# An SSM and feed-forward mix on one core: the sine tables' span angles moved into the table instructions, turns of x over two PSUM banks, and another order for emptying the last turn

## The chip, the cores and the metric

The kernel runs on one core of one Trainium2 chip. The metric is the device time of one execution in microseconds (us). One profiled execution of each kernel leaves a trace. The span in a trace is about 1.8 us shorter than the device time of the same run (214.0 against 215.83 us), since it goes from the first to the last instruction.

Engines: PE is TensorE (matmuls), DVE is VectorE, ACT is ScalarE.

## The reference

```python
def reference(x, ...):                       # x: 2048 x 640
    g = sigmoid((x * gate_w).sum(-1))
    # A: a diagonal state space model with complex poles
    Lam_bar = exp(dt * Lam)                  # dt = exp(log_dt), 640 poles
    h[t] = Lam_bar * h[t-1] + B_bar @ x[t]   # 2048 steps
    a = 2 * Re(h @ C.T) + x * Dskip
    # B: a feed-forward block, 640 -> 1728 -> 640
    b = gelu(x @ w1 + b1) @ w2 + b2
    return g * a + (1 - g) * b
```

The kernel does the scan in a rotating frame. For that it needs tables of sine and cosine of `angle * t` for t from 0 to 511, and the sine and cosine of five single angles ("spans": 1, 512, 256, 128, 64 steps; 25 columns, since the 640 poles lie in five blocks of 128) to double the tables and to carry the state between chunks.

## The kernel before

Only the opening, about the first 15 of 214 us, is touched. It must turn (transpose) the first 512 rows of x by matmuls with an identity matrix (the later rows are turned by loads that transpose). There are four row blocks of 128 rows and five column blocks each. A turn writes PSUM, and VectorE or ScalarE empties it into `xT[0]`. In between, TensorE runs strips of the first feed-forward product, into six PSUM banks. With eight banks in all, two are left for turns: `pA` and one spare.

```python
def turn_first(a, other):              # column blocks 0 and 1 of row block a
    t = bank()                         # the spare bank
    turn(t, 0, a, 0);            turned(nc.vector, t, 0, a, 0, 1)
    turn(other, a * P, a, 1);    turned(nc.scalar, other, a * P, a, 1, 2)

def turn_rest(a, t, *parts):           # column blocks 2, 3, 4 of row block a
    for k in range(KA, KD):            # KA = 2, KD = 5
        turn(t, (k - KA) * P, a, k)
    for engine, k0, k1 in parts:
        turned(engine, t, (k0 - KA) * P, a, k0, k1)

def part(kd, a):                       # a strip: six matmuls of 128 columns
    strip(kd, a * P, (a + 1) * P, kd == 0)

part(0, 0)
turn_first(1, pA)
part(1, 0)
part(0, 1)
turn_first(2, pA)
part(1, 1)
turn_first(3, pA)
part(0, 2)
turn_rest(0, bank(), (nc.scalar, KA, KD))
part(1, 2)
# ... cut: angles per step, dt and thp_c, from small columns
part(0, 3)
turn_rest(1, bank(), (nc.vector, KA, KD))
part(1, 3)
turn_rest(2, pA, (nc.scalar, KA, KD))
part(2, 0)
turn_rest(3, bank(), (nc.vector, KA, KA + 1), (nc.scalar, KA + 1, KD))
# the first 64 steps of the tables: u = t * angle, reduced to half a turn
nc.vector.tensor_tensor(out=u, in0=tf[...], in1=over(thp_c[:], HC), op=ALU.mult)
# ... cut: kk = round(u), red = u - kk
part(2, 1)
part(2, 2)
part(2, 3)
nc.scalar.activation(out=FS[:, :, 0:HC], in_=red, func=ACT.Sin, scale=TWO_PI_M)
# ... cut: cosine; then the same five steps for the 25 span angles (two, kq, redq, absq, sq, cq)
for kf in range(FA):
    for kd in (4, 3):
        ff1_mm(banks[kf], 0, kf, kd, 0, CH, False, 3)   # 512 columns each
for kf in range(FA):
    ff1_act(banks[kf], 0, kf)                           # Gelu: the table is loaded anew
```

`turn_rest(3, ...)` is the one turn that two engines empty. The first engine named goes first.

## Time and profile before

| | before |
|---|---|
| time, median of 3 runs (range) | 215.72 us (215.24 to 215.78) |
| span of the trace | 214.0 us |
| first turn / last matmul starts | 3.29 / 211.06 us |
| Sin table load / first Gelu start | 10.03 / 13.88 us |

The page's first part, of before: busy time, share of the span, number of instructions.

```profile
PE 210.5 (98%) x1407; PEld 126.5 (59%) x1407; DVE 189.4 (88%) x389; ACT 103.3 (48%) x188; POOL 1.0 (0%) x13
```

TensorE is the bound, but "busy" cannot show how well it is fed, since matmuls are pipelined and their ends overlap with the next ones' starts. The starts can. Below is the timeline of TensorE in the opening of before: start in us, busy us, line, operation, shape, count.

```profile
4.57 0.42 PE L233 MATMUL bank<-ident,xn 128*128 128x128 bf16 x2
4.79 1.18 PE L267 MATMUL bank<-xT,w1a 128*128 128x128 bf16 x12
5.80 0.28 PE L233 MATMUL bank<-ident,xn 128*128 128x128 bf16 x2
5.91 0.50 PE L267 MATMUL bank<-xT,w1a 128*128 128x128 bf16 x6
6.40 0.27 PE L233 MATMUL bank<-ident,xn 128*128 128x128 bf16 x2
6.51 0.50 PE L267 MATMUL bank<-xT,w1a 128*128 128x128 bf16 x6
7.00 0.33 PE L233 MATMUL bank<-ident,xn 128*128 128x128 bf16 x3
...
9.11 2.46 PE L267 MATMUL bank<-xT,w1a 128*128 128x128 bf16 x24
11.41 0.17 PE L404 MATMUL bank<-ident,prmB 128*128 128x18 bf16 x1
```

Line 233 is a turn, line 267 a strip. Single matmuls of 128 columns start 55.6 ns apart here once the clock is full, those of 512 columns 215.8 ns apart. So six of them from 5.91 us should let the next start at 6.24. It starts at 6.40: TensorE stood for 0.155 us. No view of waits lists this, because the pipelined ends hide it. In the same way the row of 24 (eighteen of 128 columns, six of 512, though the row is labelled by its first) takes 18 x 0.0556 + 6 x 0.2158 = 2.30 us, and 11.41 - 9.11 is just that: no wait. The two turns at 4.57 are 0.107 us apart, twice as much: the clock is still at half speed, until 5.52 us in this run.

ScalarE in before, the same columns, with the idle time ahead of an instruction and what ended it in brackets:

```profile
8.78 0.49 ACT L242 ACTIVATE xT<-bank 128x384 bf16<-128x384 f32 x1 [0.18 <-PE bank L233]
9.63 0.38 ACT L242 ACTIVATE xT<-bank 128x256 bf16<-128x256 f32 x1 [0.37 <-DVE xT L240]
10.03 1.28 ACT L392 ACT_TABLE_LOAD   x1
11.33 0.47 ACT L392 ACTIVATE hs<-gel 128x320 f32<-128x320 f32 x1
...
12.59 1.28 ACT L272 ACT_TABLE_LOAD   x1
13.88 0.69 ACT L272 ACTIVATE gel<-bank,colB 128x512 bf16<-128x512 f32 x1
```

The second line is the last turn: ScalarE waits until VectorE has taken its piece out of the same bank. VectorE in before:

```profile
9.31 0.29 DVE L240 CAST xT<-bank 128x128 bf16<-128x128 f32 x1 [0.42 <-PE bank L233]
9.52 0.48 DVE L386 TENSOR_TENSOR gel<-tf,thp_c 128x320 f32<-128x320 f32 x1
...
11.33 0.18 DVE L395 TENSOR_TENSOR two<-thp_c,spans 128x25 f32<-128x25 f32 x1
11.54 0.18 DVE L397 CAST kq<-two 128x25 int32<-128x25 f32 x1
11.76 0.18 DVE L398 TENSOR_TENSOR redq<-two,kq 128x25 f32<-128x25 f32 x1
11.97 0.18 DVE L399 SCALAR_TENSOR_TENSOR absq<-redq 128x25 f32<-128x25 f32 x1
```

The last four are the span angles, which the change takes away.

### The profile page before, as it was taken

What the parts mean: (1) busy time and instruction counts of PE and PEld (TensorE: products, weight loads), DVE (VectorE), ACT (ScalarE), POOL (GpSimd) and SP (SyncE); (2) the same over time, 40 slices, a digit from 0 to 9 for tenths busy, and PEclk for the clock granted to TensorE, in tenths of its full rate; (3) what the DMA queues carried; (4) which work ended last, traced back from release to release, by engine and by line L of the source; (5) the groups of instructions that cost most, each with busy time, mean ns of one, the idle gap of its engine ahead of it and who ended that gap; (6) DMA issues with size and microseconds to landing.
All of it is one profiled execution on the core that took longest, in us unless ns stands there. A gap on an engine that the chain in (4) does not pass through costs nothing.

```text
span 214.0 us, 3599 instructions
## 1 busy us (share of the span) xinstructions
PE 210.5 (98%) x1407; PEld 126.5 (59%) x1407; DVE 189.4 (88%) x389; ACT 103.3 (48%) x188; POOL 1.0 (0%) x13
## 2 busy tenths in 40 slices
PE   8999999999999999999999999999999999999994
PEld 5945444454475644775457777444457687676773
DVE  2599999999998999999999999999999999993153
ACT  3599956675759579203573210455683422305100
POOL 1000000000000000000000000000000000000000
PEclk9999999999999999999999999999999999999999
DMA  6879999999000000052000006100000000110011
GB/s 192 222 178 190 201 156 246 347 207 230 1 0 0 3 0 0 14 152 96 0 0 3 0 0 180 68 0 2 3 0 14 0 3 31 61 34 0 0 66 61
DMA packets 31571, 15.84 MB, mean 74 GB/s; under 512 B 22978, under 2 KB 31554, under 8 KB 31554
## 3 DMA queue, kind: packets, MB, share of 16 engines
q1 hardware_dynamic: 30850, 14.99, 29.7%
q10 hardware_dynamic: 704, 0.62, 0.9%
q8 instruction: 11, 0.18, 0.4%
q14 instruction: 6, 0.05, 0.1%
HBM read 7.48 MB, written 2.62 MB: 47 GB/s over the span
## 4 chain that ended last, share of the span: by engine, by line
PE 98%; DVE 0%; issue 0%
PE bank L267 27%; PE bank L614 27%; PE bank L673 20%; PE bank L555 20%; PE bank L230 1%; PE bank L630 1%; PE bank L293 1%; PE bank L233 1%; DVE ot L678 0%; PE bank L362 0%; PE bank L283 0%; PE bank L404 0%; PE bank L373 0%
## 5 line engine op out<-in xcount | busy, mean ns | idle before, releaser
L614 PE MATMUL bank<-w_sb,gel 128*128 128x384 bf16 (+1 forms) x416 | 57.9, 300 | 0.0
L614 PEld LDWEIGHTS <-gel 128*128 128x128 bf16 x416 | 40.2, 98 | 17.1 <-issue 0.8
L558 ACT ACTIVATE bu<-bank 128x512 bf16<-128x512 f32 x40 | 23.7, 606 | 37.6 <-PE bank L555 37.6
L272 ACT ACTIVATE gel<-bank,colB 128x512 bf16<-128x512 f32 x52 | 33.6, 695 | 10.5 <-PE bank L267 10.2
L673 PEld LDWEIGHTS <-hs 128*128 128x128 bf16 x330 | 31.7, 98 | 11.7
L509 DVE TENSOR_TENSOR_SCAN g<-r_c,carry,v 128x512 bf16<-128x512 f32 x30 | 37.2, 1270 | 0.0
L622 ACT ACTIVATE gb<-bank,gcol 128x384 f32<-128x384 f32 (+1 forms) x32 | 15.1, 526 | 32.8 <-PE bank L614 16.6
L267 PE MATMUL bank<-xT,w1a 128*128 128x512 bf16 (+1 forms) x174 | 28.5, 319 | 0.0
L673 PE MATMUL bank<-CT_im,hs 128*128 128x320 bf16 (+2 forms) x165 | 27.1, 295 | 0.0
L673 PE MATMUL bank<-CT_re,hs 128*128 128x320 bf16 (+2 forms) x165 | 27.1, 295 | 0.0
L678 DVE SCALAR_TENSOR_TENSOR ot<-bank,gcol,gb 128x320 bf16<-128x320 f32 (+2 forms) x33 | 17.4, 533 | 9.8 <-PE bank L673 9.5
L555 PE MATMUL bank<-xT,BT_re 128*128 128x512 bf16 x100 | 24.9, 379 | 0.0
L555 PE MATMUL bank<-xT,BT_im 128*128 128x512 bf16 x100 | 24.9, 379 | 0.0
L267 PEld LDWEIGHTS <-w1a 128*128 128x128 bf16 x174 | 14.9, 101 | 11.6
L267 PE MATMUL bank<-xT,w1b 128*128 128x512 bf16 x80 | 17.9, 379 | 0.0
L555 PEld LDWEIGHTS <-BT_im 128*128 128x128 bf16 x100 | 9.8, 98 | 11.8
L588 DVE TENSOR_TENSOR bank<-xn,Dbc 128x320 f32<-128x320 bf16 (+2 forms) x33 | 14.5, 482 | 2.1 <-ACT gb L622 2.1
L555 PEld LDWEIGHTS <-BT_re 128*128 128x128 bf16 x100 | 9.6, 98 | 11.0
L490 DVE TENSOR_TENSOR v<-wa,wb 128x512 bf16<-128x512 bf16 x40 | 15.2, 421 | 0.6
L603 ACT ACTIVATE bank<-b2bc 128x384 f32<-128x384 bf16 (+1 forms) x24 | 11.7, 526 | 7.6 <-DVE ot L678 7.6
L490 DVE TENSOR_TENSOR wa<-TCOS,g 128x1024 bf16<-128x1024 bf16 x20 | 13.7, 686 | 0.1
L267 PE MATMUL bank<-xT,w1c 128*128 128x512 bf16 x60 | 13.7, 379 | 0.0
(103 smaller groups left out, 167.8 us busy)
## 6 DMA issues: line engine op xcount, KB each, us to landing
out_dram<-ot SPq DMA_DIRECT2D x15, 160.0 KB, 1.8
w_sb<-in_B_w_dram SPq DMA_DIRECT2D x1, 2080.0 KB
xn<-in_A_x_dram SPq DMA_DIRECT2D x3, 640.0 KB
w1b<-in_B_w_dram SPq DMA_DIRECT2D x5, 128.0 KB, 3.8
w1c<-in_B_w_dram SPq DMA_DIRECT2D x5, 112.0 KB, 4.3
w1a<-in_B_w_dram ACTq DMA_DIRECT2D x2, 192.0 KB, 3.0
w1a<-in_B_w_dram SPq DMA_DIRECT2D x1, 384.0 KB, 3.5
xn<-in_A_x_dram SPq DMA_DIRECT2D x4, 64.0 KB, 3.7
```

Of the source, the lines that this page charges most:

```text
L267: nc.tensor.matmul(p[:, t0:t1], lhsT=w, rhs=xT[c][:, kd, t0:t1], start=(kd == 0) if first is None else first, stop=(kd == last), skip_grou ...
L272: nc.scalar.activation(out=gel[c][:, kf, :], in_=p[:, :], func=ACT.Gelu_apprx_tanh, bias=b1_c[:, kf:kf + 1])
L490: nc.vector.tensor_tensor(out=o, in0=a, in1=b, op=op)
L509: nc.vector.tensor_tensor_scan(s["g"][:, ri, :], r_c[:, ks:ks + 1].to_broadcast([P, CH]), s["v"][:, ri, :], init, ALU.mult, ALU.add)
L555: nc.tensor.matmul(p[:], lhsT=BT[ks >= KSA][:, kd, (ks % KSA if ks < KSA else ks - KSA) * P:][:, 0:P], rhs=xT[c][:, kd, :], start=(kd == 0 ...
L558: nc.scalar.activation(out=bu[:, ri, :], in_=p[:], func=ACT.Identity)
L588: dve_now(ck.pe, 0.45, lambda: nc.vector.tensor_tensor(out=p[:, 0:d1 - d0], in0=xn[c][:, a, d0:d1], in1=Dbc[:, d0:d1], op=ALU.mult))
L603: nc.scalar.activation(out=v, in_=src, func=ACT.Identity)
L614: nc.tensor.matmul(p[:, col:col + d1 - d0], lhsT=gel[c][:, kf, a * P:(a + 1) * P], rhs=w2_sb[:, kf, d0:d1], start=False, stop=False, skip_ ...
L622: nc.scalar.activation(out=gbs[ti][:, d0:d1], in_=p[:, col:col + d1 - d0], func=ACT.Identity, scale=gcol[:, 1, ti:ti + 1])
L673: nc.tensor.matmul(p[:, 0:d1 - d0], lhsT=hs[c][:, j, lo:lo + P], rhs=CT[:, j % KS, d0:d1], start=False, stop=(j == 2 * KS - 1), skip_group ...
L678: nc.vector.scalar_tensor_tensor(out=ot[:, d0:d1], in0=p[:, 0:d1 - d0], scalar=gcol[:, 0, ti:ti + 1], in1=gbs[ti][:, d0:d1], op0=ALU.mult, ...
```

## The change

Its intent: the 25 span angles need no instructions of their own when they ride as five more columns in the tables' instructions; turns that alternate over the two banks wait less for a bank; and when ScalarE empties the last turn first, it can load its Sin table sooner, and so the Gelu table after it.

```diff
-    spans = const.tile([P, NQ], F32, name="spans")
+    NP = NQ + HC                                  # 5 + 64 columns
+    tf = const.tile([P, NP], F32, name="tf")
...
-    FSC = hsp.tile([P, 2 * KS, HB], F32, name="hs")
+    FSC = hsp.tile([P, 2 * KS, NQ + HB], F32, name="hs")
...
     part(1, 0)
+    turn_first(2, pA)
     part(0, 1)
-    turn_first(2, pA)
     part(1, 1)
     turn_first(3, pA)
     part(0, 2)
-    turn_rest(0, bank(), (nc.scalar, KA, KD))
     part(1, 2)
...
+    turn_rest(0, bank(), (nc.scalar, KA, KD))
     part(0, 3)
-    turn_rest(1, bank(), (nc.vector, KA, KD))
+    turn_rest(1, pA, (nc.vector, KA, KD))
     part(1, 3)
-    turn_rest(2, pA, (nc.scalar, KA, KD))
+    turn_rest(2, bank(), (nc.scalar, KA, KD))
     part(2, 0)
-    turn_rest(3, bank(), (nc.vector, KA, KA + 1), (nc.scalar, KA + 1, KD))
     nc.vector.tensor_tensor(out=u, ...)           # now 5 x 69 columns
+    turn_rest(3, pA, (nc.scalar, KA + 1, KD), (nc.vector, KA, KA + 1))
...
-    # five steps and two Sin activations for the 25 span angles
...
+    for dst, r in ((sq, 0), (cq, 1)):             # the spans out of the tables
+        nc.vector.tensor_copy(out=dst[...], in_=FSC[:, r * KS:(r + 1) * KS, 0:NQ])
```

More of the change, by code (lines that the diff above doesn't have):

```diff
@@ L166 @@
     NQ = 5
-    spans = const.tile([P, NQ], F32, name="spans")
+    NP = NQ + HC
+    tf = const.tile([P, NP], F32, name="tf")
     for i, m in enumerate((1.0, float(CH), float(CH // 2), float(CH // 4), float(CH // 8))):
-        nc.gpsimd.memset(spans[:, i:i + 1], m)
+        nc.gpsimd.memset(tf[:, i:i + 1], m)
     nc.sync.dma_start(out=b1x[:, 0:F_LAST], in_=B_b1[F - F_LAST:F].rearrange("(o d) -> o d", o=1).to_broadcast([P, F_LAST]))
@@ L224 @@
     nc.vector.memset(halfpi[:], HALF_PI)
-    tf = const.tile([P, HC], F32, name="tf")
-    nc.vector.tensor_copy(out=tf[:], in_=tfi[:])
+    nc.vector.tensor_copy(out=tf[:, NQ:NP], in_=tfi[:])
     ones = lambda n: nc.const_aps.tensor(1.0, [P, n], BF16)
@@ L337, in scratch @@
     def scratch(i):
-        return scr[:, i * KS * P:i * KS * P + KS * HC].rearrange("p (k i) -> p k i", k=KS)
+        return scr[:, i * KS * P:i * KS * P + KS * NP].rearrange("p (k i) -> p k i", k=KS)
     u, red, ab = scratch(0), scratch(1), scratch(2)
-    FSC = hsp.tile([P, 2 * KS, HB], F32, name="hs")
-    FS = FSC[:, 0:KS, :]
-    FC = FSC[:, KS:2 * KS, :]
-    two = col("two", n=NQ * KS)
-    kq = col("kq", I32, n=NQ * KS)
-    redq = col("redq", n=NQ * KS)
-    absq = col("absq", n=NQ * KS)
+    FSC = hsp.tile([P, 2 * KS, NQ + HB], F32, name="hs")
+    FS = FSC[:, 0:KS, NQ:NQ + HB]
+    FC = FSC[:, KS:2 * KS, NQ:NQ + HB]
     sq = col("sq", n=NQ * KS)
     cq = col("cq", n=NQ * KS)
-    kk = work.tile([P, KS, HC], I32, name="bu", bufs=8)
+    kk = work.tile([P, KS, NP], I32, name="bu", bufs=8)
     sth, cth = sq[:, 0:KS], cq[:, 0:KS]
@@ L379 @@
     nc.vector.tensor_tensor(out=thp_c[:], in0=dt16[:], in1=limp[:], op=ALU.mult)
-    turn_rest(1, bank(), (nc.vector, KA, KD))
+    turn_rest(1, pA, (nc.vector, KA, KD))
     nc.scalar.activation(out=r_c[:], in_=dtl[:], func=ACT.Exp)
     part(1, 3)
-    turn_rest(2, pA, (nc.scalar, KA, KD))
+    turn_rest(2, bank(), (nc.scalar, KA, KD))
     part(2, 0)
-    turn_rest(3, bank(), (nc.vector, KA, KA + 1), (nc.scalar, KA + 1, KD))
-    nc.vector.tensor_tensor(out=u, in0=tf[:].rearrange("p (o i) -> p o i", o=1).to_broadcast([P, KS, HC]), in1=over(thp_c[:], HC), op=ALU.mult)
+    nc.vector.tensor_tensor(out=u, in0=tf[:].rearrange("p (o i) -> p o i", o=1).to_broadcast([P, KS, NP]), in1=over(thp_c[:], NP), op=ALU.mult)
+    turn_rest(3, pA, (nc.scalar, KA + 1, KD), (nc.vector, KA, KA + 1))
     nc.vector.tensor_copy(out=kk[:], in_=u)
@@ L391 @@
     part(2, 3)
-    nc.scalar.activation(out=FS[:, :, 0:HC], in_=red, func=ACT.Sin, scale=TWO_PI_M)
+    nc.scalar.activation(out=FSC[:, 0:KS, 0:NP], in_=red, func=ACT.Sin, scale=TWO_PI_M)
     nc.vector.scalar_tensor_tensor(out=ab, in0=red, scalar=-1.0, in1=red, op0=ALU.mult, op1=ALU.max)
-    nc.scalar.activation(out=FC[:, :, 0:HC], in_=ab, func=ACT.Sin, scale=-TWO_PI_M, bias=halfpi[:])
-    nc.vector.tensor_tensor(out=two[:].rearrange("p (n k) -> p n k", n=NQ), in0=thp_c[:].rearrange("p (o k) -> p o k", o=1).to_broadcast([P, NQ, KS]),
-                            in1=spans[:].rearrange("p (n o) -> p n o", o=1).to_broadcast([P, NQ, KS]), op=ALU.mult)
-    nc.vector.tensor_copy(out=kq[:], in_=two[:])
-    nc.vector.tensor_tensor(out=redq[:], in0=two[:], in1=kq[:], op=ALU.subtract)
-    nc.vector.scalar_tensor_tensor(out=absq[:], in0=redq[:], scalar=-1.0, in1=redq[:], op0=ALU.mult, op1=ALU.max)
-    nc.scalar.activation(out=sq[:], in_=redq[:], func=ACT.Sin, scale=TWO_PI_M)
-    nc.scalar.activation(out=cq[:], in_=absq[:], func=ACT.Sin, scale=-TWO_PI_M, bias=halfpi[:])
+    nc.scalar.activation(out=FSC[:, KS:2 * KS, 0:NP], in_=ab, func=ACT.Sin, scale=-TWO_PI_M, bias=halfpi[:])
     for kf in range(FA):
@@ L429, in double @@
         nc.vector.tensor_tensor(out=FS[:, :, hi], in0=m1, in1=m2, op=ALU.add)
+    for dst, r in ((sq, 0), (cq, 1)):
+        nc.vector.tensor_copy(out=dst[:].rearrange("p (n k) -> p k n", n=NQ), in_=FSC[:, r * KS:(r + 1) * KS, 0:NQ])
     double(HC, 4)
```

## The prediction

> **What bounds the kernel now.** TensorE: the page gives it 98% of the 214.0 us span, and the chain of waits that ended last is 98% PE. In the timeline, matmul starts are 216 ns apart for 512 columns and 56 ns for 128, without a wait from 9.1 us to the last matmul at 211.1 us. The waits are all in the opening. At 3.98 us the first strip waits 0.16 us for the first turned tile. Four times a turn waits for the one spare PSUM bank to be emptied: 0.155 us before 6.40, 0.152 before 7.00, 0.046 before 7.91, 0.032 before 8.94; in sum 0.39 us. Matmuls before 5.5 us run at half speed (107 ns per 128 columns). The Trainium skill, "TensorE: Matmul & The Clock Gate", Part 1, calls this a warm-up whose window is free-running, so it differs between runs; the trace agrees with the two spacings. The change does not touch it.
>
> **What the change does.**
> - VectorE: four 25-element instructions go (0.18 us each), two 25-element copies come (estimated 0.2 us each), four instructions grow from 320 to 345 elements (about 0.03 us each). Net about -0.3 us, off the chain.
> - ScalarE: two Sin activations of 25 elements (0.2 and 0.3 us) go; two grow slightly.
> - Turns alternate over the spare bank and pA, and one first-turn moves ahead of a strip. My estimate from the trace's latencies (0.26 us from a turn's matmul to its evacuation, 0.05 us from there to the next matmul): the waits before the last first-turn and turns 0, 1 and 3 vanish; turn 2 still waits about 0.1 us for ScalarE to empty turn 0. Gain about 0.3 us by the last turn, whose matmuls start at about 8.65 instead of 8.94 us.
> - The last turn's two evacuations swap. They read one bank, and the second waits for the first (the Trainium skill, "PSUM — Partial Sum Buffer", section "PSUM bank collisions raise a hardware error"; in the trace ScalarE idles 0.37 us until VectorE is done). ScalarE now goes first, at about 9.0 us, and the Sin table load starts at about 9.4 instead of 10.03 us. But VectorE's piece of that turn is done only at about 9.7 us (before: 9.60), and the last 128-column strip, which could now start at 9.48 (before: 9.78), waits about 0.28 us for it. This gives back nearly all of the gain.
>
> **Sin and Gelu earlier.** First Gelu at about 13.05 instead of 13.88 us. TensorE does not wait for it: its bank was free at 14.57 and needed at 14.89 us. So this earns nothing by itself; it keeps that slack.
>
> **Sum.** Bank waits -0.3 us, strip wait +0.28 us: net about -0.05 us, uncertain by 0.25. Predicted 215.6 us, range 215.1 to 216.0. Chances: faster by over 2% 0.005, within 2% 0.99, slower 0.005.
>
> **What would show it.** In the timeline: no gap before the last first-turn and turn 0; a gap of 0.2 to 0.3 us before the last 128-column strip; the 512-column matmuls after it start near 10.1 us as before; first Gelu near 13.0; no gaps after that.
>
> **What would make it wrong.** Another warm-up phase (a few tenths); the x tile for the third first-turn, which landed at 5.31 us and is now wanted at 5.4, arriving late; no wait at the last strip, which would leave 0.3 us of gain; the tables' new 261-column stride slowing VectorE enough to reach TensorE.

## The result

| | before | after |
|---|---|---|
| time, median of 6 runs (range) | 215.75 us (215.24 to 216.55) | 215.61 us (215.43 to 216.12) |
| ratio after / before, 95% interval | | 0.9994 (0.9972 to 1.0017) |
| span of the trace | 214.0 us | 213.7 us |
| last matmul starts | 211.06 us | 210.72 us |
| Sin table load / first Gelu start | 10.03 / 13.88 us | 9.09 / 12.68 us |

By the times the two kernels are the same.

The traces tell a tempting tale: the Gelu comes 1.2 us sooner, and the span is 0.35 us shorter. The lines of after that answer those above, the page first:

```profile
PE 210.0 (98%) x1407; PEld 126.1 (59%) x1407; DVE 189.0 (88%) x387; ACT 103.2 (48%) x186; POOL 1.0 (0%) x13
```

TensorE in after, from the timeline:

```profile
4.58 0.28 PE L233 MATMUL bank<-ident,xn 128*128 128x128 bf16 x2
4.69 0.50 PE L267 MATMUL bank<-xT,w1a 128*128 128x128 bf16 x6
5.18 0.27 PE L233 MATMUL bank<-ident,xn 128*128 128x128 bf16 x2
5.29 0.83 PE L267 MATMUL bank<-xT,w1a 128*128 128x128 bf16 x12
5.96 0.28 PE L233 MATMUL bank<-ident,xn 128*128 128x128 bf16 x2
...
8.48 2.75 PE L267 MATMUL bank<-xT,w1a 128*128 128x128 bf16 x24
11.07 0.17 PE L393 MATMUL bank<-ident,prmB 128*128 128x18 bf16 x1
```

Two things differ. At 4.58 us the clock is already full (six matmuls fit between 4.69 and 5.18, with 0.155 us to spare, which is a wait for the bank). And the row of 24 now takes 11.07 - 8.48 = 2.59 us where its work is 2.30: a wait of 0.29 us inside it. The chain of waits, in order of time, says for what (start, us, what):

```profile
8.48 0.18 PE bank L233 x3
8.68 0.39 ACT xT L242
9.08 0.02 issue
9.10 0.30 DVE xT L240
9.40 0.04 issue
9.45 1.79 PE bank L267 x12
```

The path leaves TensorE here: last turn, ScalarE's piece, VectorE's piece, and only then the last strip, at 9.45 us. In before the chain never left TensorE in the opening; there the last turn and what follows read:

```profile
9.07 0.20 PE bank L233 x3
9.27 2.30 PE bank L267 x24
```

ScalarE and VectorE in after:

```profile
8.18 0.89 ACT L242 ACTIVATE xT<-bank 128x384 bf16<-128x384 f32 x2 [0.32 <-PE bank L233]
9.09 1.28 ACT L388 ACT_TABLE_LOAD   x1
...
11.38 1.28 ACT L272 ACT_TABLE_LOAD   x1
12.68 1.84 ACT L272 ACTIVATE gel<-bank,colB 128x512 bf16<-128x512 f32 x3
```

```profile
8.11 0.51 DVE L381 TENSOR_TENSOR gel<-tf,thp_c 128x345 f32<-128x345 f32 x1
9.10 0.29 DVE L240 CAST xT<-bank 128x128 bf16<-128x128 f32 x1 [0.48 <-ACT xT L242]
...
11.73 0.18 DVE L421 COPY sq<-hs 128x25 f32<-128x25 f32 x1
11.81 0.17 DVE L421 COPY cq<-hs 128x25 f32<-128x25 f32 x1
```

VectorE now idles 0.48 us for ScalarE where ScalarE idled 0.37 us for VectorE. The Trainium skill, "PSUM — Partial Sum Buffer", section "PSUM bank collisions raise a hardware error", says that two engines on one bank collide, reads against reads too. At the last turn the two traces show them kept apart: ScalarE starts at 9.63 us in before, VectorE's piece having begun at 9.31 and taken 0.29; VectorE starts at 9.10 us in after, ScalarE having ended at 9.07. No run here lets them meet.

### The profile page after: what moved, and what is told of

It reads as the page before. It is cut to its first block, busy times and chain, and to the rows that moved or that the text cites. A ratio compares the mean times of both kernels' runs of the same rounds, so it can differ in the third digit from the quotient of the medians.

```text
span 213.7 us, 3596 instructions
## 1 busy us (share of the span) xinstructions
PE 210.0 (98%) x1407; PEld 126.1 (59%) x1407; DVE 189.0 (88%) x387; ACT 103.2 (48%) x186; POOL 1.0 (0%) x13
## 4 chain that ended last, share of the span: by engine, by line
PE 98%; DVE 0%; ACT 0%; issue 0%
PE bank L605 27%; PE bank L267 26%; PE bank L664 20%; PE bank L546 20%; PE bank L230 1%; PE bank L621 1%; PE bank L293 1%; PE bank L233 1%; ACT xT L242 0%; DVE ot L669 0%; PE bank L358 0%; DVE xT L240 0%; PE bank L283 0%; PE bank L393 0%; PE bank L368 0%
## 5 line engine op out<-in xcount | busy, mean ns | idle before, releaser
L481 DVE TENSOR_TENSOR wa<-TCOS,g 128x1024 bf16<-128x1024 bf16 x20 | 13.7, 685 | 0.1
L267 PE MATMUL bank<-xT,w1c 128*128 128x512 bf16 x60 | 13.7, 379 | 0.0
```

What stands on the lines that cost most here:

```text
L267: nc.tensor.matmul(p[:, t0:t1], lhsT=w, rhs=xT[c][:, kd, t0:t1], start=(kd == 0) if first is None else first, stop=(kd == last), skip_grou ...
L481: nc.vector.tensor_tensor(out=o, in0=a, in1=b, op=op)
```

## Where the 0.35 us between the two spans comes from

From the starts of all matmuls, every profiled run can be taken apart into four terms: when the first turn starts; how much longer the matmuls after it are apart while the clock is at half speed ("cold"); how long TensorE stands beyond that ("waits", gaps of over 20 ns at full clock); and the rest. Worked out for before, after and the four experiments of the first set below, in us:

| run | first turn | cold, until | waits | last matmul | rest |
|---|---|---|---|---|---|
| before | 3.29 | 0.96, 5.52 | 0.55 | 211.06 | 206.27 |
| after | 3.34 | 0.46, 4.58 | 0.66 | 210.72 | 206.27 |
| vector_first | 3.28 | 0.20, 3.71 | 0.41 | 210.16 | 206.27 |
| angles_only | 3.28 | 0.54, 4.65 | 0.71 | 210.79 | 206.26 |
| gelu_late_1 | 3.28 | 1.02, 5.72 | 0.66 | 211.23 | 206.27 |
| gelu_late_2 | 3.29 | 1.52, 6.70 | 1.86 | 212.94 | 206.27 |

The rest is the last matmul's start less the other three, and it is the same to 0.01 us in all six. (It also holds eight gaps of 0.09 to 0.10 us, before and after each of the four groups of 64-row matmuls, line 630 in before. They are over 20 ns too, but alike in all six runs; so the prediction's "without a wait from 9.1 us" is not quite so.) So nothing after the opening differs but the two waits for the Gelu in the gelu_late runs, and the account is complete. It says that after, as profiled, waited 0.11 us *more* than before. It was shorter because its clock was full 0.9 us sooner, which saved 0.50 us. The cold term is not the kernel's doing: it went from 0.20 to 1.52 us over these runs, although all six issue the same matmuls in the same order up to the end of the second strip, at 4.8 to 5.4 us, and in three of them the clock was full before that.

The waits depend on the clock too. With a clock that is full early, the strips are short and there is less to hide an evacuation behind. So before and after have to be compared under the same clock.

## The experiments

My theory: the alternating banks save about 0.3 us of waits, the swap at the last turn gives 0.29 us back, and the earlier tables earn nothing. Rival A: the earlier Sin and Gelu tables are the gain, the 0.3 us of the spans is real, and scatter hides it in the times. Rival B: all of this is off the path, in both directions.

In the first set of four, the kernel before of the same rounds had a median of 215.81 us (11 runs).

### vector_first: the order at the last turn undone

```diff
-    turn_rest(3, pA, (nc.scalar, KA + 1, KD), (nc.vector, KA, KA + 1))
+    turn_rest(3, pA, (nc.vector, KA, KA + 1), (nc.scalar, KA + 1, KD))
```

> The changed kernel with one thing undone: VectorE empties its piece of the last turn first, then ScalarE. My theory (the bank gain is eaten by the last strip's wait for VectorE's piece): the gap of 0.29 us before the last 128-column strip goes, the Sin table load starts at about 9.4 instead of 9.09 us, first Gelu near 13.0, no new gap, about 0.29 us less than the changed kernel for the same warm-up. Rival A (the earlier Sin table and Gelu are what the change earns, and the span fell 0.3 us for that): giving up 0.3 us of the early table costs about 0.3 us. Rival B (all of the opening is off the path): no change in gaps or in time.

Measured: 215.6 us median (214.88 to 216.28, 6 runs), ratio to before 0.9993 (0.9973 to 1.0012), which settles nothing. The trace does. TensorE and then ScalarE of vector_first, from the timeline:

```profile
8.21 2.46 PE L267 MATMUL bank<-xT,w1a 128*128 128x128 bf16 x24
10.51 0.17 PE L393 MATMUL bank<-ident,prmB 128*128 128x18 bf16 x1
```

```profile
8.73 0.38 ACT L242 ACTIVATE xT<-bank 128x256 bf16<-128x256 f32 x1 [0.34 <-DVE xT L240]
9.14 1.28 ACT L388 ACT_TABLE_LOAD   x1
...
12.71 1.84 ACT L272 ACTIVATE gel<-bank,colB 128x512 bf16<-128x512 f32 x3
```

The row of 24 is back to 10.51 - 8.21 = 2.30 us. The gap is gone and no other came; the waits are 0.41 us against 0.66 of after. That is 0.25 and not 0.29 less, since the first strip, which starts at 3.98 us either way, stands 0.05 us longer when the clock is full before it. The table came at 9.14 rather than my 9.4 us, and the first Gelu at 12.71 rather than near 13.0, because this run's clock was full earliest of all. Its span of 213.1 us is 0.6 us below that of after, of which 0.25 is waits and 0.26 the luck of the clock (0.05 more is the first turn). Rival B falls by the trace: an order of two evacuations moved 0.29 us.

### angles_only: only the span angles, turns as before

The diff of the change without its lines on `turn_first` and `turn_rest`.

> The kernel before with only the span angles put into the table instructions; turns as before. My theory: VectorE about 0.3 us less busy, first Gelu some 0.4 us earlier than before, the four bank waits of before stay (sum 0.39 us), no gap at the last strip, time within 0.1 us of before. Rival A: 0.1 to 0.3 us faster than before, since Gelu comes sooner.

Measured: 215.81 us median (215.44 to 216.38, 6 runs), ratio 1.0011 (0.9992 to 1.0031). The four bank waits stand in the trace (0.154, 0.154, 0.047, 0.034 us), no gap at the last strip. The first Gelu came at 13.34 us, 0.54 before that of before, but 0.27 of this is the clock's: the last turn was 0.27 us sooner too. But there is a fifth wait that I had not seen in before: 0.155 us ahead of a strip at 5.20 us, which waits for the turned tile. This run's clock was full at 4.65 us; in before the same strip ran cold, and the wait was hidden. So under an early full clock before waits 0.71, and after 0.66 us.

### gelu_late_1 and gelu_late_2: the tables later on purpose

```diff
+    for _ in range(2):                            # gelu_late_2: 4
+        nc.scalar.activation(out=idle[:], in_=idle[:], func=ACT.Identity)   # 128x512
     nc.scalar.activation(out=FSC[:, 0:KS, 0:NP], in_=red, func=ACT.Sin, scale=TWO_PI_M)
```

> The changed kernel with two idle ScalarE instructions of 128x512 (about 0.57 us each) put ahead of its Sin instructions, about 1.1 us in sum: Sin about 0.9 to 1.1 us later, first Gelu at about 13.7. My theory: the first freed bank is needed only at 14.55 us and is still free by about 14.4, so no matmul waits; same time as the changed kernel within 0.1 us. Rival A: the early table is the gain, so it costs about 0.3 us or more.

> The same with four idle instructions, about 2.3 us: first Gelu at about 14.9, first bank free at about 15.6, needed at 14.55. My theory: now the slack is gone and TensorE waits about 1.0 us before the 512-column matmuls of the ninth row block; 0.9 to 1.1 us slower than the changed kernel. Rival A: 2 us slower or more (every us of lateness costs), or in proportion to gelu_late_1.

gelu_late_1: 215.98 us median (215.58 to 216.2, 6 runs), ratio 1.0009 (0.9994 to 1.0024). My number for the first Gelu was a miss: it started at 14.32, not 13.7 us, since an idle instruction took 0.65 us rather than 0.57 and the clock of this run was full only at 5.72 us. So it used up all of the slack, and TensorE waited for it by 0.033 us, at 15.06. By the times alone, which scatter over 0.6 us, rival A would not be excluded; by the trace, a Gelu 1.64 us later than in after cost 0.033 us (the late clock helped: the bank was needed at 15.03 us, 0.48 later than in after). (This run also waited 0.126 us for the small load ahead of the angles, which no other run did.)

gelu_late_2: 216.97 us median (216.57 to 217.7, 6 runs), ratio 1.0061 (1.0043 to 1.0080). TensorE, then ScalarE:

```profile
13.25 2.32 PE L269 MATMUL bank<-xT,w1b 128*128 128x512 bf16 x10
16.77 1.46 PE L269 MATMUL bank<-xT,w1b 128*128 128x512 bf16 x6 [1.20 <-ACT gel L274]
```

```profile
9.82 2.62 ACT L391 ACTIVATE idle<-idle 128x512 f32<-128x512 f32 x4
...
16.03 2.42 ACT L274 ACTIVATE gel<-bank,colB 128x512 bf16<-128x512 f32 x4
```

By starts the wait is 16.77 - 13.25 - 10 x 0.2158 = 1.36 us (the bracket says 1.20, as it counts from the modelled end). I had expected 1.0; the longer idle instructions make the difference. In both runs the matmul starts 0.05 us after the first Gelu ends, and not a moment is lost before that. This is a limit, not a slope: in before the first bank was free at 14.57 and needed at 14.89 us; in after at 13.37 and 14.55. The earlier tables raise the slack from 0.3 to 1.2 us, and slack is all that they give. Rival A falls.

### The gated four: the same kernels with the warm-up taken out

To see a few hundredths of a us in the times, the clock's luck had to go. The turns' identity matrix is copied by ScalarE behind thirteen idle instructions, and thirty more warm-up matmuls run meanwhile. The real work then starts at 12.64 us with its loads landed (I had expected about 11 us, and 7 to 8 us more time in sum; it was 8.6 us more).

```diff
+    for _ in range(13):
+        nc.scalar.activation(out=idle[:], in_=idle[:], func=ACT.Identity)
+    nc.scalar.activation(out=gated[:], in_=ident[:], func=ACT.Identity, bias=idle[:, 0:1])
+    for _ in range(30):
+        nc.tensor.matmul(pA[:, 0:512], lhsT=ones(P), rhs=ones(512), start=True, stop=True)
...
-                         rhs=ident[:], ...)        # in turn()
+                         rhs=gated[:], ...)
```

> The kernel before with its opening held back: thirteen idle ScalarE instructions pass before the turns' identity matrix is copied, and thirty more 512-column matmuls warm TensorE's clock, so that the real work starts at about 11 us with a full clock and its data long there. Some 7 to 8 us longer than the kernel before. It takes the warm-up's chance out of the time. Expected: no matmul of the real work at half speed; waits as in angles_only (one strip 0.155, turns 0.154, 0.154, 0.047, 0.034 us, and the first strip), and run times closer together than without the gate.

> The changed kernel with the same gate. My theory: its waits sum to 0.05 us less than those of gated_before, so its time is within 0.15 us of gated_before (0.05 us faster). Rival A (the 0.3 us between the two profiled spans is what the change earns): 0.3 us faster than gated_before. Rival C (the gain is real but only with a cold start): 0.0.

> The changed kernel with VectorE first in the last turn, gated. My theory: the strip's wait of 0.29 us is gone, 0.29 us faster than gated_after and 0.34 us faster than gated_before. Rival A: slower than gated_after by up to 0.3 us, since the Sin table comes later; rival B (the opening is off the path): the same as both.

> The kernel before with only the span angles in the table instructions, gated. My theory: the same waits and the same time as gated_before within 0.1 us, with the first Gelu some 0.5 us earlier relative to the start of the real work. Rival A: 0.1 to 0.3 us faster.

| run | times of the runs at full clock, us | granted clock | waits after the first turn, us |
|---|---|---|---|
| gated_before | 224.50, 224.50 | 1.000 | (its trace is of a slower run) |
| gated_angles_only | 224.46, 224.47, 224.50, 224.50 | 1.000 | 0.86 |
| gated_after | 224.41, 224.42, 224.45, 224.46, 224.47 | 1.000 | 0.81 |
| gated_vector_first | 224.15, 224.16, 224.16, 224.18 | 1.000 | 0.51 |

The gate failed in part. Three of five runs of gated_before (225.69 to 225.73) and one of gated_angles_only (225.68) ran at a granted clock of 0.992: the clock fell back to half speed in the opening, as the one of them that was profiled shows. They are left out here, a choice made after the times were seen; the ratios to the ungated kernel before (1.0434, 1.0398, 1.0385, 1.0411) contain them and say only that a gate costs time. With that, gated_before rests on two runs, and its waits were not seen at full clock; gated_angles_only, which has the same turns, stands beside it. What I expected of the first Gelu of gated_angles_only (0.5 us before that of gated_before) can't be checked for the same reason. And the first strip, whose wait is part of the sums in the table, waits 0.32 us in all four traces and not 0.16, since the three filler matmuls between the first turn and it now run at full clock.

The rest of the runs of each kernel agree within 0.06 us, where the ungated ones scatter over 0.6 to 1.4 us. After is 0.05 us faster than before (224.45 against 224.50). That is no more than the spread of one kernel's runs, and before has two of them; what carries it is that the waits in the traces say the same (0.81 against 0.86). The rest is clear by the times alone. vector_first is 0.29 us faster than after and 0.34 us faster than before. The span angles alone change nothing (224.485 against 224.50, medians). The first Gelu of gated_after came at 21.68 us, that of gated_vector_first at 21.98: the faster kernel has the later tables. Rival A expected the opposite sign. Rival C (a gain with a cold start only) is not borne out by the traces either: in the run whose clock filled last, gelu_late_2, the waits other than that for the Gelu are 1.86 - 1.36 = 0.50 us, and before, with a late clock too, has 0.55: again 0.05 us.

TensorE's first turn in gated_before and in gated_after, from the timeline:

```profile
12.64 0.27 PE L242 MATMUL bank<-gated,xn 128*128 128x128 bf16 x2 [2.28 <-ACT gated L237]
```

```profile
12.65 0.27 PE L242 MATMUL bank<-gated,xn 128*128 128x128 bf16 x2 [1.50 <-ACT gated L237]
```

In gated_before the warm-up matmuls were done sooner, as the clock had filled sooner, and TensorE stood longer at the gate. By starts it stood 2.44 us there; half speed followed from 14.3 to 17.7 us. In the three profiled runs that stood 1.33 to 1.93 us, none followed.

## Why the prediction was right

- **The time**: 215.6 predicted, 215.61 us measured. That match is better than it deserves: a run scatters by several tenths with the clock. What deserves trust is the net of -0.05 us, which the gated runs show as such.
- **The last strip waits about 0.28 us for VectorE's piece**: 0.292 us in the trace; 0.29 us in the gated times when only this order is undone.
- **The bank waits fall by about 0.3 us**: under an early full clock, the kernel with before's turns (angles_only) waits 0.54 us after its first strip has started, and vector_first, which has the new turns without the swap, 0.20 us: 0.34 us less. In the gated times it is 0.34 us. Under a late clock it is as much: the turns wait 0.39 us in before and 0.05 us in gelu_late_2.
- **Turn 2 still waits about 0.1 us**: 0.048 us.
- **One term I had wrong**: I saw only a late x tile as a danger to the third first-turn. It waited 0.155 us for the spare bank at 5.18 us (not for x: gated, with x long there, it waits as long). I had costed that stretch with the half-speed matmuls of before's trace, behind which the evacuation fits; with an early full clock it does not. The same clock gives before another wait of the same size (angles_only, at 5.20 us), so the net was not moved. That these two waits cancel is luck: the prediction had neither. Under the late clock that it was worked out for, neither is there (gelu_late_2), and its sum holds term by term.
- **The tables earn nothing**: shown by gelu_late_1, gelu_late_2 and the gated pair. All my times for ScalarE in after were some 0.3 us late, because the clock in after's trace was full 0.9 us sooner.
- **VectorE about 0.3 us less busy**: 0.4 us (189.4 to 189.0). The copies took 0.18, not 0.2 us, and the tables' 261-column stride cost nothing that the trace shows (the 256-column steps 348 and 484 ns, as before).

The version that beats both is vector_first. In the ordinary kernel the times cannot confirm its 0.34 us (ratio 0.9993, 0.9973 to 1.0012); the trace and the gated runs do. The 0.16 us wait of the first strip and the 0.155 us one after the second turn are still there.

## What to carry to other kernels

When two engines empty one bank, ask which of the pieces the bound engine needs first and let that engine go first; a table load that nobody waits for is no reason to go ahead of it. An earlier event only earns what the bound engine waited for it, so look for the moment at which its result is needed before counting its earliness as gain. And when a difference is smaller than the scatter, take the matmul starts of each trace apart into work, half-speed clock and waits before believing that the shorter span is the change.

## What the Trainium skill lacked or had wrong

- "TensorE: Matmul & The Clock Gate", Part 1, puts the transition to full clock at around 4 us of sustained matmuls, within 500 ns from run to run. In these six ungated traces it came 2.9 to 5.9 us after the first matmul (at 3.71 to 6.70 us, the first matmul at 0.77). The page's free-running window and its "don't fit to a specific cold count" agree; its figure for the cost (under 1% of a span) holds too, 0.20 to 1.52 us of 214 after the first turn, but this is up to five times what the change's parts are worth.
- The same page, same part, has the clock fall after at least one idle window of about 3.4 us. In gated_before TensorE stood only 2.44 us between matmuls, and half speed followed 1.6 us after it had resumed, for 3.4 us. So a wholly idle window of that length was not needed in this trace; standing 1.93 us or less did not do it in the other three. The clock in this trace changes at 4.00, 14.24 and 17.65 us, 3 x 3.413 and 3.413 us apart. If its windows lie on that grid, which is an inference, TensorE stood 2.29 of the 3.41 us before the fall (1.82, 0.32 and 0.16), and at most 1.52 us in any such window of the other three openings.
- "ScalarE: Activation LUTs", section "What ACT_TABLE_LOAD costs", gives about 1283 ns for the load and about 1380 ns of drain, 2.66 us for a switch. The load was 1283 ns here, but from the end of the activation before it to the start of the one after it a switch took 1.31 us (10.015 to 11.328 us in before); no drain shows.
- No page says that a wait of TensorE of 0.05 to 0.3 us can be missing from the list of waits, though "Perfetto Trace Analysis" calls the end of a matmul an estimate. The modelled end lies 0.16 us after its successor could start (379 ns of duration at 215.8 ns of spacing), and the list leaves short gaps out: of the last strip's 0.29 us, 0.13 remain and are not listed, while the gated first strip's 0.32 us appears as 0.15. Only the starts show it.
